# Denser cells, and the last two feed-forward groups in three float32r parts, in a fused mLSTM and feed-forward kernel

## The chip, the cores and the metric

One core of one Trainium2 chip runs the whole kernel in one launch. The metric is device time in microseconds (us). The core's engines are TensorE (PE; its weight loads are listed apart as PEld), VectorE (DVE), ScalarE (ACT), GpSimd (POOL) and SyncE (SP), which here issues nearly all DMAs. Each engine works through its own queue in order.

## The reference

```python
def _attn_ref(q, k, v, i_gate, f_gate, o_gate):          # q, k, v, o: (4, 8, 768, 40); gates: (4, 8, 768)
    for t in range(S):
        m_new = np.maximum(f_gate[:, :, t] + m, i_gate[:, :, t])
        f_stab = np.exp(f_gate[:, :, t] + m - m_new)
        i_stab = np.exp(i_gate[:, :, t] - m_new)
        m = m_new
        C = f_stab[:, :, None, None] * C + i_stab[:, :, None, None] * np.einsum('bhd,bhe->bhde', vt, kt)
        n = f_stab[:, :, None] * n + i_stab[:, :, None] * kt
        h_tilde = np.einsum('bhde,bhe->bhd', C, qt)
        denom = np.maximum(np.abs(np.einsum('bhd,bhd->bh', n, qt)[:, :, None]), 1.0)
        y[:, :, t] = 1.0 / (1.0 + np.exp(-o_gate[:, :, t])) * h_tilde / denom

def _moe_ref(x, w_in, w_out):                            # x: (3072, 320), w_in: (320, 2048), w_out: (2048, 320)
    h = x @ w_in
    g = np.maximum(0.01 * h, h)
    return (g @ w_out).astype(np.float32)
```

The cell's output, transposed to tokens by 8 x 40 features, is x. All is float32, except that the two weights come as float64.

## The kernel before

The sequence of 768 is cut into six chunks of 128 tokens (c = 0 to 5). With four batches (B = 4) there are 24 steps, s = 4 c + b. Inside a chunk the recurrence is worked in parallel form: decay weights (`gates`, `gates_exp`, `prep_mask`, `prep_exp`), scores and state products (`u_parts`), and the outputs (`u_plain` in chunk 1, `u_mix` in chunks 2 to 5). `u_mix` ends with VectorE transposes, a GpSimd multiplication and four DMAs that write the step's x, transposed, to memory (`x_dr`); `gather_x` reads it back in the layout that the feed-forward needs, with features on the partitions: two halves of 64 partitions and five slots (`SLOTS`), so that two row halves of TensorE can run side by side.

The feed-forward group g works on the 4 x 128 tokens of chunk g: `ff_units(g)` gives 32 pieces. The first 16 are half-units of the input product (`rows`, L743: products of 64 rows x 128 weight columns with 512 token columns into `ph`; ScalarE's Prelu, L751, writes `acts`). The last 16 are `part(n, m)` (L778: four products of 128 x 128 with 320 columns into `po`; after the fourth part ScalarE copies `po` out, L786, and a DMA stores it). All these products are float32. Weights arrive as 64-bit words and are narrowed by ScalarE and VectorE (`narrow_weights`, L231 to L247) in chunk 1.

The order of the work on TensorE, VectorE, ScalarE and GpSimd is the program's own order (a manual schedule); SP's DMAs are ordered by the framework, which also inserts all waits. After `first_chunk`, the loop over c = 1 to 6 goes through the 32 pieces of group c - 1 and puts the cells of chunk c between them: in chunks 2 to 5 at the pieces in

```python
        pairs = (2, 2, 6, 6, 14, 14, 19, 19, 19)
```

that is `u_parts` of two steps behind piece 2, their `u_mix` behind piece 6, the next two steps behind 14 and 19. After a `u_mix`, `ahead(s + 2)` prepares a later step (VectorE's `prep_kq`, GpSimd's `prep_vu`, DMAs for the step after it), `feed(s + NL)` loads the step that reuses its buffers, and from the middle of the group on `gather_x` runs. `masks` sets where GpSimd adds the causal mask (`prep_mask`, L434). Group 5 runs alone at the end, since there are no more cells.

Of the kernel before, what the change touches and what calls it, by code (L numbers as in the profile page):

```python
# [9 lines left out]
F32 = mybir.dt.float32  # L10
U32 = mybir.dt.uint32
# [3 lines left out]
PSUM = bass.MemoryType.PSUM  # L15


@with_exitstack
def kernel(
# [51 lines left out]
    assert KR == DP and KC == 5 and KC * DP == Dm and GT * 4 <= 2048  # L71

    consts = ctx.enter_context(tc.tile_pool(name="consts", bufs=1))
    gp = ctx.enter_context(tc.tile_pool(name="gates", bufs=1))
    wk = ctx.enter_context(tc.tile_pool(name="wk", bufs=2))
    psf = ctx.enter_context(tc.tile_pool(name="psf", bufs=4, space=PSUM))
    psc = ctx.enter_context(tc.tile_pool(name="psc", bufs=4, space=PSUM))
# [38 lines left out]
    NL = 4  # L116
# [8 lines left out]
    acts = consts.tile([P, NF, GT], F32, name="acts")  # L125
# [36 lines left out]
    QN = NF // 4  # L162
    QC = 4 * P
    WC = KC * 2 * P
    w_in = consts.tile([P, QN, WC], F32, name="w_in")
    w_out = consts.tile([P, NF, Dm], F32, name="w_out")
# [5 lines left out]
    def w_row(r, slot, j):  # L172
        n, e = divmod(j, 2)
        at = (2 * slot + e) * P
        return w_in[DP * r : DP * (r + 1), n, at : at + P]
# [6 lines left out]
    HW = 2 * Dm  # L182
    wide = moe_w_in.dtype == U64
    raws = {}
    if wide:
        raw_t = consts.tile([P, 5 * HW], U64, name="raw")

    def load_weights(n):

        m = n - QN  # L190
        if n < QN:
            dst = w_in[:, n, :]
        else:
            dst = w_out[:, 2 * m : 2 * m + 2, :].rearrange("p a d -> p (a d)")
        to = dst
        if wide:
            if n < 2:
                at = NF * GT - 2 * WC * (n + 1)
                raw = acts_l[:, at : at + 2 * WC].bitcast(U64)
            elif n < QN:  # L200
                raw = raw_t[:, WC * (n - 2) : WC * (n - 1)]
            elif m < 2:
                raw = w_out[:].rearrange("p f d -> p (f d)")[:, (2 + m) * WC : (3 + m) * WC].bitcast(U64)
            else:
                at = (4, 0, 1, 2, 3, 4)[m - 2] * HW
                raw = raw_t[:, at : at + HW]
            raws[n] = (raw, dst)
            to = raw
# [11 lines left out]
    def narrow_weights(n):  # L220
# [3 lines left out]
        if not wide:  # L224
            return
# [491 lines left out]
    def u_x(s):  # L717
# [3 lines left out]
        if b == 0:  # L721
            st["xT", c] = wk.tile([P, KC, GT], F32, name="xT", bufs=1)
# [308 lines left out]
```

## Time and profile before

| | us |
|---|---|
| median of 3 runs (lowest, highest) | 528.52 (527.25, 528.54) |
| profiled execution: its span from the first to the last instruction (the page gives it no other time) | 526.4 |
| TensorE busy in the span | 513.2 |
| VectorE, ScalarE, GpSimd busy | 240.3, 168.1, 113.0 |
| start of group 1's first product | 139.64 |
| start of group 5's first product | 453.96 |

A row of the page's fifth part, or of the groups by line, reads: line, engine, operation, written tile <- read tiles, shape, count | busy us, mean ns of one | idle time of the engine just before them, and who ended it. Durations of single instructions on TensorE overlap each other; what they cost in a row is read from the chain of waits, where the pieces stand in order of time with their start and length.

### The profile page before, as it was taken

What the parts mean: (1) busy time and instruction counts of PE and PEld (TensorE: products, weight loads), DVE (VectorE), ACT (ScalarE), POOL (GpSimd) and SP (SyncE); (2) the same over time, 40 slices, a digit from 0 to 9 for tenths busy, and PEclk for the clock granted to TensorE, in tenths of its full rate; (3) what the DMA queues carried; (4) which work ended last, traced back from release to release, by engine and by line L of the source; (5) the groups of instructions that cost most, each with busy time, mean ns of one, the idle gap of its engine ahead of it and who ended that gap; (6) DMA issues with size and microseconds to landing.
All of it is one profiled execution on the core that took longest, in us unless ns stands there. A gap on an engine that the chain in (4) does not pass through costs nothing.

```text
span 526.4 us, 11333 instructions
## 1 busy us (share of the span) xinstructions
PE 513.2 (97%) x4501; PEld 336.3 (64%) x4501; DVE 240.3 (46%) x431; ACT 168.1 (32%) x458; POOL 113.0 (21%) x145
## 2 busy tenths in 40 slices
PE   8889989999999999999999999999999999999997
PEld 7877878777555577555577555577554577544675
DVE  4679998999328446028445028344028230000000
ACT  4565865534534212034212124212125100122100
POOL 4244354152205121015021015021013010000000
PEclk9668999999999999999999999999999999999999
DMA  9977687888755626685626676626542112000000
GB/s 116 156 204 153 138 212 171 196 145 175 146 137 105 137 72 150 129 174 107 138 75 143 134 150 129 138 76 155 125 102 52 50 52 87 14 0 1 12 12 25
DMA packets 165284, 59.13 MB, mean 112 GB/s; under 512 B 128816, under 2 KB 156016, under 8 KB 165232
## 3 DMA queue, kind: packets, MB, share of 16 engines
q1 hardware_dynamic: 164848, 58.28, 51.0%
q8 instruction: 35, 0.57, 0.5%
q10 hardware_dynamic: 384, 0.13, 0.1%
q14 instruction: 17, 0.14, 0.1%
HBM read 51.68 MB, written 6.70 MB: 111 GB/s over the span
## 4 chain that ended last, share of the span: by engine, by line
PE 83%; SPq 6%; DVE 4%; DMA 2%; ACT 2%; issue 1%; POOL 1%; ACTq 0%; POOLq 0%
PE po L778 38%; PE ph L743 36%; PE pT L679 3%; SPq L213 3%; PE sd L598 3%; SPq L338 2%; SPq L352 1%; PE sd L603 1%; DMA rb<-in_q_dram 1%; DVE raw L245 1%; DVE qn L608 1%; DMA S<-in_v_dram 0%; DMA raw<-in_moe_w_in_dram 0%; PE tk L518 0%; PE hN L649 0%
## 5 line engine op out<-in xcount | busy, mean ns | idle before, releaser
L743 PE MATMUL ph<-xT,w_in 64*128 64x512 f32 (+1 forms) x1120 | 215.2, 536 | 0.6 <-ACT acts L751 0.6
L778 PE MATMUL po<-w_out,acts 128*128 128x320 f32 x768 | 211.1, 434 | 0.0
L778 PEld LDWEIGHTS po<-w_out,acts 128*128 128x128 f32 x768 | 144.5, 190 | 62.6 <-issue 4.1
L743 PEld LDWEIGHTS ph<-xT,w_in 64*128 64x128 f32 x1120 | 107.8, 189 | 94.4 <-issue 87.7
L751 ACT ACTIVATE acts<-ph 128x512 f32<-128x512 f32 (+1 forms) x112 | 53.9, 534 | 151.8 <-PE ph L743 151.7
L608 DVE TENSOR_TENSOR qn<-w,sd 64x512 f32<-64x512 f32 x40 | 27.4, 684 | 97.7 <-PE sd L603 57.1
L576 POOL TENSOR_TENSOR S<-S,f 40x336 f32<-40x336 f32 x36 | 30.9, 858 | 101.9 <-PE pT L679 65.8
L442 ACT ACTIVATE w<-w,gT 128x64 f32<-128x64 f32 (+1 forms) x192 | 51.1, 348 | 3.1 <-POOL w L434 2.1
L434 POOL TENSOR_TENSOR w<-w,i 128x512 f32<-128x512 f32 x20 | 28.1, 1411 | 104.7 <-ACT bu L294 53.0
L786 ACT COPY y<-po 128x320 f32<-128x320 f32 x12 | 5.1, 423 | 83.3 <-PE po L778 83.3
L786 ACT COPY hn<-po 128x320 f32<-128x320 f32 x12 | 5.1, 426 | 76.0 <-PE po L778 76.0
L686 DVE STREAM_TRANSPOSE hb<-pT 128x512 f32<-128x512 f32 x16 | 11.4, 714 | 39.2 <-PE pT L679 39.0
L495 DVE TENSOR_TENSOR qn<-kqT,ea 64x512 f32<-64x512 f32 x32 | 27.3, 854 | 0.9
L693 POOL TENSOR_TENSOR xb<-xb,den 128x320 f32<-128x320 f32 x16 | 11.7, 728 | 66.5 <-DVE xb L690 66.5
L598 PEld LDWEIGHTS sd<-kqT 40*64 40x64 f32 x640 | 19.9, 135 | 6.1 <-issue 6.1
L697 DVE STREAM_TRANSPOSE x<-xb 128x512 f32<-128x512 f32 x16 | 18.1, 1130 | 7.7 <-POOL xb L693 7.7
L598 PE MATMUL sd<-kqT 40*64 40x64 f32 x640 | 21.5, 220 | 0.0
L603 PE MATMUL sd<-S,vu 64*40 64x42 f32 x576 | 20.1, 214 | 0.7 <-POOL vu L462 0.7
L489 DVE STREAM_TRANSPOSE kqT<-rb 128x512 f32<-128x512 f32 x32 | 20.5, 677 | 0.0
L603 PEld LDWEIGHTS sd<-S,vu 64*40 64x40 f32 x576 | 18.6, 111 | 0.8 <-POOL vu L462 0.8
L580 DVE TENSOR_TENSOR S<-S,sd 40x336 f32<-40x336 f32 x36 | 18.1, 503 | 1.0
L679 PEld LDWEIGHTS pT<-qn,S 128*64 128x64 f32 x512 | 15.6, 138 | 3.6 <-issue 3.5
(126 smaller groups left out, 364.9 us busy)
## 6 DMA issues: line engine op xcount, KB each, us to landing
w<-a_dr SPq DMA_DIRECT2D x40, 128.0 KB
rb<-in_k_dram SPq DMA_DIRECT2D x64, 80.0 KB
rb<-in_q_dram SPq DMA_DIRECT2D x64, 80.0 KB
rb<-in_o_gate_dram SPq DMA_DIRECT2D x64, 80.0 KB
ea<-a_dr SPq DMA_DIRECT2D x32, 128.0 KB
kn<-in_k_dram SPq DMA_DIRECT2D x24, 160.0 KB
raw<-in_moe_w_out_dram SPq DMA_DIRECT2D x6, 640.0 KB
S<-in_v_dram SPq DMA_DIRECT2D x80, 40.0 KB
```

The source lines that it names most:

```text
L434: nc.gpsimd.tensor_tensor(w, w, cm2.unsqueeze(1).to_broadcast([P, H, SL]), op=ALU.add)
L442: yield nc.scalar.activation(w[:, h, :], w[:, h, :], AF.Exp, bias=gT[c][:, 0, bh : bh + 1], scale=1.0)
L489: nc.vector.transpose(d["kqT"][:, i].rearrange("p (h t n) -> p h n t", n=TS, t=QW), raw_blocks(s, i, QW).rearrange("p (h n) d -> p h n d", ...
L495: nc.vector.tensor_tensor(mixed(s)[rows, 1 - r], d["kqT"][rows, 1].rearrange("p (h t) -> p h t", t=SL), d["ea"][rows], op=ALU.mult,)
L576: nc.gpsimd.tensor_tensor(new, old, g, op=ALU.mult)
L598: nc.tensor.matmul(bank[1 - u][toks, h, :], lhsT=kqT[rows, 0, ts(h, SL)], rhs=kqT[rows, 1, ts(h, SL)], start=True, stop=True,)
L603: nc.tensor.matmul(dC[u][:, h].rearrange("p k d -> p (k d)"), lhsT=d["ku"][toks, h], rhs=S_v[s % NL][toks, u, h, :, :V1], start=True, stop ...
L608: nc.vector.tensor_tensor(mixed(s)[toks, u], w[toks], bank[1 - u][toks], op=ALU.mult)
L679: nc.tensor.matmul(pT[DP * r : DP * (r + 1), j * P + u * SL : j * P + (u + 1) * SL], lhsT=S[:, u, h, :], rhs=m[:, u, h, :], start=True, st ...
L743: nc.tensor.matmul(ph[r][:, cols], lhsT=w_row(r, slot, j), rhs=xT[DP * r : DP * (r + 1), slot, cols], start=(slot == 0), stop=(slot == KC ...
L751: nc.scalar.activation(acts[:, f, cols], ph[r][:, cols], AF.Prelu, alpha=0.01)
L778: nc.tensor.matmul(po[n][:], lhsT=acts[:, f, ts(n, P)], rhs=w_out[:, f, :], start=(f == 0), stop=(f == NF - 1),)
```

## The change

Four things are changed.

1. Cells of chunks 2 to 5 come among 24 pieces (`UC`) instead of 32, at (2, 2, 7, 7, 13, 13, 18, 18, 18). The pieces of groups 1 to 3 are simply counted on, so 96 pieces hold four chunks; in chunk 5 the loop ends behind piece 18, and the last five pieces of group 3 follow without cells. `gather_x` goes to other places.
2. v is loaded by one DMA instead of four, into the tile of the decay weights `w`, and GpSimd copies it from there into `S` (two copies in `prep_mask`). The spread of the weights (`spread`, `spread_q`) is one DMA instead of two each.
3. When the cells are done their tiles are given up, and groups 4 and 5 are worked as four half-groups (hg 8 to 11) of 256 tokens, in units of two row blocks (8 units a half-group, `enter` and `leave`). x and w_in, and from hg 9 on also the activations and w_out, are written as three float32r tensors each: a number is split by a bit mask into a high part and a rest, and three products (v = 0, 1, 2) into two PSUM sums are joined afterwards (`JOIN`).
4. The weights are split by `split_w`, in halves of 640 columns: one quarter of w_in in chunk 3, the other seven quarters (three of w_in, four of w_out) from the last five pieces of group 3 on, in steps between the units of hg 8. Two units' products are issued in a row: `enter(u)`, `enter(u + 1)`, then `leave(u - 2)`, `leave(u - 1)`.

```diff
-        for u in range(2):
-            for i in range(2):
-                nc.sync.dma_start(S_v[n][ts(u, SL), u, :, i, :DB], v[b, :, ...].rearrange("h p d -> p h d"))
+        w = wk.tile([P, H, P], F32, name="w", bufs=NL)[:].rearrange("p h t -> p (h t)")
+        ...
+        nc.sync.dma_start(w[:, H * SL : H * SL + Dm].rearrange("p (h d) -> p h d", d=D), v[b, :, rows, :].rearrange("h p d -> p h d"))
...
         w = st[s]["w"]
+        for u in range(2):
+            nc.gpsimd.tensor_copy(S_v[s % NL][ts(u, SL), u, :, :, :DB], st[s]["v"][ts(u, SL)])
         nc.gpsimd.tensor_tensor(w, w, cm2.unsqueeze(1).to_broadcast([P, H, SL]), op=ALU.add)
...
-        pairs = (2, 2, 6, 6, 14, 14, 19, 19, 19)
+        pairs = (2, 2, 7, 7, 13, 13, 18, 18, 18)
+        UC = 24
+
+        def split_w(w, parts):
+            tmp = raw_b[:].bitcast(F32)
+            n = WC // 2
+            for i in range(2):
+                at = slice(n * i, n * (i + 1))
+                h, low = (tmp[:, n * (2 * i + k) : n * (2 * i + k + 1)] for k in range(2))
+                nc.vector.tensor_scalar(h.bitcast(U32), w[:, at].bitcast(U32), scalar1=HIGH, scalar2=None, op0=ALU.bitwise_and)
+                yield
+                nc.scalar.copy(parts[0][:, at], h)
+                nc.gpsimd.tensor_tensor(low, w[:, at], h, op=ALU.subtract)
+                yield
+                nc.scalar.activation(parts[1][:, at], low, AF.Copy, scale=SPLIT)
+                yield
+                nc.vector.scalar_tensor_tensor(parts[2][:, at], in0=low, scalar=SPLIT, in1=h, op0=ALU.mult, op1=ALU.subtract)
+                yield
...
+        for c in range(2, NB):
+            cells, done, fed = cell_units(c), 0, 0
+            for i in range(UC):
+                ...
+                if c == 3:
+                    if i == 2:
+                        now = split_in(0)
+                    if i >= 2 and i % 2 == 0:
+                        run(now, 1)
+                ffs[at]()
+                at += 1
+                ...
+                visits(c, i)
+                ...
+                if c == NB - 1 and i == pairs[-1]:
+                    break
+
+        cell.close()
...
+        def split_x(hg):
+            to = xs[hg % 2]
+            for at, n in ((0, 3), (3, 2)):
+                ...
+                nc.vector.tensor_scalar(h.bitcast(U32), x.bitcast(U32), scalar1=HIGH, scalar2=None, op0=ALU.bitwise_and)
+                nc.scalar.copy(to[0][:, at : at + n, :], h)
+                nc.gpsimd.tensor_tensor(to[1][:, at : at + n, :], x, h, op=ALU.subtract)
+                nc.vector.scalar_tensor_tensor(to[2][:, at : at + n, :], in0=h, scalar=JOIN, in1=x, op0=ALU.mult, op1=ALU.subtract)
+                yield
...
+        load_x(HG0)
+        first = split_x(HG0)
+        now = splits()
+        while at < len(ffs):
+            ffs[at]()
+            at += 1
+            run(first, 1)
+            run(now, 4)
...
+        def enter(u):
+            ...
+            ph = psh.tile([P, 2, 2, GH], F32, name="p3")          # two buffers
+            for v in range(3):
+                for slot in range(KC):
+                    for r in range(2):
+                        nc.tensor.matmul(ph[:, r, v // 2, :], lhsT=w[rows, v, c0 : c0 + P], rhs=x[v][rows, slot, :], ...)
+            nc.scalar.activation(a, ph[:, :, 0, :], AF.Copy, scale=JOIN)
+            nc.vector.tensor_tensor(a, a, ph[:, :, 1, :], op=ALU.add)
+            nc.scalar.activation(a, a, AF.Prelu, alpha=0.01)
+
+        def grow(u):
+            ...
+            nc.vector.tensor_scalar(h.bitcast(U32), a.bitcast(U32), scalar1=HIGH, scalar2=None, op0=ALU.bitwise_and)
+            nc.scalar.copy(g[:, 0], h)
+            nc.vector.tensor_tensor(g[:, 1], a, h, op=ALU.subtract)
+            nc.vector.scalar_tensor_tensor(g[:, 2], in0=h, scalar=JOIN, in1=a, op0=ALU.mult, op1=ALU.subtract)
+
+        def leave(u):
+            # hg 8: one float32 product of 320 columns for each of 2 token halves and 2 row blocks;
+            # hg 9 to 11: three float32r products each; after a half-group's last unit the sums are joined and stored
+            ...
+
+        for u in range(HG0 * NJ, HG2 * NJ + LAG, 2):
+            hg, j = divmod(u, NJ)
+            for i in range(2):
+                if HG1 * NJ < u <= HG2 * NJ:
+                    grow(u - 2 + i)
+            for i in range(2):
+                if hg < HG1:
+                    run(now, 8)
+                if u < HG2 * NJ:
+                    enter(u + i)
+            if hg + 1 < HG2:
+                if j == 2:
+                    first = split_x(hg + 1)
+                if j in (2, 4):
+                    run(first, 1)
+                if j == 4 and hg + 2 < HG2:
+                    run(first, 1)
+                    load_x(hg + 2)
+            for i in range(2):
+                if u >= HG0 * NJ + LAG:
+                    leave(u - LAG + i)
```

## The prediction

> **What bounds the kernel now.** The page first, then the chain of waits in order of time, then groups by shape, single lines with their shortest, median and longest instruction, and the timelines of VectorE and GpSimd where the cells end.
>
> ```profile
> PE 513.2 (97%) x4501; PEld 336.3 (64%) x4501; DVE 240.3 (46%) x431; ACT 168.1 (32%) x458; POOL 113.0 (21%) x145
> PE   8889989999999999999999999999999999999997
> DVE  4679998999328446028445028344028230000000
> PEclk9668999999999999999999999999999999999999
> ```
>
> TensorE is the bound: full in every slice from the ninth on. VectorE's zeros at the right end are the room that the change wants to use.
>
> ```profile
> 139.64 7.07 PE ph L743 x32
> ...
> 218.46 7.07 PE ph L743 x32
> ...
> 375.99 7.07 PE ph L743 x32
> ...
> 427.99 26.04 PE po L778 x96
> 454.03 34.53 PE ph L743 x160
> 488.56 34.66 PE po L778 x128
> ```
>
> This is the chain. A group with a chunk's cells among its pieces takes 218.46 - 139.64 = 78.8 us, the one with the last chunk 454.03 - 375.99 = 78.0. A group alone takes 34.53 + 34.66 = 69.2: 16 half-units of ph and 16 parts of po at 2.16 us. So cells cost TensorE 9.6 us a chunk (the last 8.85), and the last matmul ends 526.4 - 523.2 = 3.2 us before the end. Moving cells among pieces gains TensorE nothing; it has to be given cheaper products.
>
> ```profile
> L778 PE MATMUL po<-w_out,acts 128*128 128x320 f32 x768 | 211.1, 434 | 0.0
> L743 PE MATMUL ph<-xT,w_in 64*128 64x512 f32 x800 | 176.3, 593 | 0.0
> L434 POOL TENSOR_TENSOR w<-w,i 128x512 f32<-128x512 f32 x20 | 28.1, 1411 | 104.7 <-ACT bu L294 53.0 <-DMA w<-a_dr 50.7 <-ACT w L442 1.0
> L243 DVE TENSOR_SCALAR raw<-w_out x6: 495/500/898, 94.0 to 126.8; 128x640 uint32<-128x640 uint32 x6
> L241 DVE SCALAR_TENSOR_TENSOR w_out<-raw,w_out x6: 824/825/1775, 92.2 to 125.9; 128x640 uint32<-128x640 uint32 x6
> L434 POOL TENSOR_TENSOR w<-w,i x20: 1262/1274/1764, 51.5 to 389.8; 128x512 f32<-128x512 f32 x20
> ```
>
> These are the prices. The two counts, 768 and 800, are twice the products written: a float32 product is two instructions. Without overlap a po product of 320 columns takes 34.66 / 64 = 542 ns and a ph product of 512 columns 34.53 / 80 = 432 (two row halves run side by side).
>
> ```profile
> 429.06 0.73 POOL L693 TENSOR_TENSOR xb<-xb,den 128x320 f32<-128x320 f32 x1 [23.28 <-DVE xb L690]
> 433.05 0.73 POOL L693 TENSOR_TENSOR xb<-xb,den 128x320 f32<-128x320 f32 x1 [3.27 <-DVE xb L690]
> 433.81 1.10 DVE L697 STREAM_TRANSPOSE x<-xb 128x512 f32<-128x512 f32 x1 [0.84 <-POOL xb L693]
> ```
>
> After the last cell matmul (427.99) VectorE still works until 434.9. GpSimd starts 0.08 to 0.14 us after VectorE hands over, VectorE 0.03 after GpSimd.
>
> **Part 1, when the cells are done (T0).** Up to 139.6 little changes. v comes by one DMA for four and the spread by one for two, against two GpSimd copies per step (nearest row 0.73, 1.5 a step). TensorE idles 3.4 us between 40 and 140, so the gain is at most 3.4; four uncovered steps would lose 6. I take 0. Behind that, 91 pieces and four chunks' cells: 139.6 + 3 x 69.2 - 5 x 2.17 + 3 x 9.63 + 8.85 = 374.1 = T0, against 428.0 before. The work per chunk is as before, in about 61.5 us instead of 78.8. VectorE needs 13 us for a pair of u_mix (316.2 to 329.2) and the next u_parts comes six pieces (13.0 us) later: just enough. SP issued without a pause from 353.0 to 386.5 behind a pair of u_mix; without four v DMAs, two spreads and most gathers that is some 22. I take 1 us in all, bounds 0 and 20 (5 a chunk).
>
> **Part 2, the products.** No row shows float32r. The nearest is the float32 product, two instructions; three float32r products cost between 3/4 of it (a quarter each, 54 ns for a ph product of 256 columns, 135 for po) and 3/2 (half each, what one of the two instructions takes); three times a whole one is the far end. I take a quarter. Then a unit of two row blocks takes 30 x 54 = 1.62 us in and 12 x 135 = 1.63 out, where float32 takes 2.16 each; a half-group takes 13.0 for 17.3. Nothing waiting, from T0: five pieces 10.8, hg 8 13.0 + 17.3 (its output stays float32), hg 9 to 11 26 each, together 119.1, and the span 374.1 + 119.1 + 3.2 = 496.4. That is the 30 us that the change is after.
>
> The trace hides the 128-row weight loads (190 ns) wholly behind products of the same rows: two po instructions take the 542. The Trainium skill, "TensorE: Matmul & The Clock Gate", part 3 "What overlaps and what doesn't", says that a load overlaps a running matmul only where their row groups differ, which speaks against short products. By it, with its 107 ns a load, an output product would be an estimated 242 for 135 and the whole up to 31 us later (107 ns x 12 x 24 units); the rows contradict it, and I keep the 135. "FP8 and Floating Point Precision", "TensorE Precision Notes", gives true FP32 four passes and lets reduced FP32 be truncated; one pass would be the quarter, and no row here shows it.
>
> **Part 3, the splitting, which decides.** A weight quarter is split in two halves of 640 columns: VectorE masks (0.50, L243), GpSimd subtracts (1.274 x 640/512 = 1.59, L434), VectorE joins (0.83, L241). In the order that the changed program issues, the next mask stands behind the join on VectorE's queue and the join waits for GpSimd. So a half takes 0.50 + 1.59 + 0.83 + 0.16 of hand-overs = 3.1 us, one after another. ScalarE's two copies (0.79 each, L231) fit beside. w_in's first quarter is split in chunk 3; seven quarters, 14 halves, are left at T0, and VectorE comes to them 6.9 us later, behind the last u_mix. x's two pieces come in between: 0.59 + 0.99 + 0.40 + 0.66, and GpSimd's part of them holds the halves up some 0.5: 3.2.
>
> The first add out of PSUM (0.69) has x and seven halves before it on VectorE, the next three two more each. ScalarE's scaled copy (0.59, L751) also stands in program order behind the halves; with the add it is 1.3. The adds end at T0 + 6.9 + 3.2 + 21.7 + 1.3 = 33.1, then, 6.2 + 1.3 later each, at 40.6, 48.1 and 55.6. PSUM has two buffers for enter, so units 66 to 69 wait for just these adds: behind the stalled enter stand all later products, and TensorE, which would be at unit 66 after 14 us, idles. After the fourth add TensorE still has enter(69) 1.6, two leaves 4.3, two enters 3.2, two leaves 4.3, two enters 3.2, two leaves 4.3, to T0 + 76.7; with nothing waiting this point is 10.8 + 13.0 + 17.3 + 3.2 = 44.3. Loss 32.
>
> **Part 4, hg 9 to 11.** A round of two units costs TensorE 6.5. VectorE does twice mask 0.43, subtract 0.69, join 0.69 and add 0.69 (512 columns; L608 and L495 0.69). Its second add waits for ScalarE's activation and next scaled copy of 0.59 each, in ScalarE's order: 3.6 + 0.69 + 0.59 + 0.59 + 0.69 + 0.5 of hand-overs = 6.65. Twelve rounds are 79.8, two further x splits 5.3, output adds 2.9: 88 against TensorE's 75. The gain of these products, 13, is eaten by the engine that prepares them.
>
> **The sum.** 374.1 + 76.7 + 88.0, then copy, add and store 3.7 (3.2 plus an add of 0.5): 542.5; 1 for part 1 and 2 for x's tiles, which reuse memory whose last stores may still be on their way (0 to 3). Span 545.5. The page gives the profiled execution by its span alone, 526.4; the median run is 528.5, 2.1 above. So 548.
>
> **Rivals.**
> *The preparing engines keep up.* Order and counts are fixed; open is only the price of a half, since no row subtracts two plain tensors of 640 columns on GpSimd. From T0 on 171 us are forecast (3 of them for parts 1 and 2) and 152.3 would be break-even: 13 halves would have to take 1.6 us each instead of 3.1. With the subtraction at nothing they take 1.4, TensorE is through hg 8 at T0 + 55, and the span 524, time 526; if the rounds of part 4 then also go at TensorE's 6.5, 514 and 516. Against it: L434's shortest of 20 is 1262 ns for fewer columns, and the mask and the join alone are 1.3. Faster by over 0.3%, 0.10 (about 500 to 526); between, 0.02.
> *float32r at half a float32 product.* Unit 3.24 in, 3.25 out, a round 13: TensorE bounds again. T0 + 84, twelve rounds 156, 3.7: 618, time 620; at the far end near 790. 0.09.
> *The dense cells starve TensorE.* 5 us a chunk: 565 to 570. 0.07.
> *The forecast,* 536 to 562 (a half at 2.8 to 3.4 is 4 either way, hand-overs in part 4 another 6, part 1 -3 to +6): 0.72.
>
> The range, 530 to 582, holds the forecast and the starving with something for their sum; the two outer rivals, 0.19, stay outside. 0.3% (1.6 us) is about what a measurement of this kernel tells from no change: faster 0.10, same 0.02, slower 0.88.
>
> **What would show it.** Right: the u_mix of chunk 5 ends near 374; behind it TensorE has some 15 us of idle time ended by VectorE's add, then 6 us gaps; VectorE is idle between mask and join, released by GpSimd; there a granted clock below 1.0, as PEclk's second and third slices have (0.6); VectorE at 9 tenths and more in the last 90 us. Wrong: if products of 256 columns follow each other at over 60 ns in the middle of a unit, part 2 fails; if the 14 halves last under 30 us, part 3 fails; if group 1 to 3 pieces show gaps, part 1.

## The result, and the profile after

| | before | after |
|---|---|---|
| median us (lowest, highest) | 528.53 (527.25, 529.76) | 651.00 (650.49, 653.68) |
| ratio after / before (95% interval) | | 1.233 (1.229 to 1.237) |
| span of the profiled execution, us | 526.4 | 651.9 |
| mean granted TensorE clock in it | 0.976 | 0.895 |
| last product of a cell ends (T0), us | 427.99 | 479.45 |
| from there to the end of the span, us | 98.4 | 172.4 |

The change costs 23%. The forecast was 548, with 582 as the upper end. Its two halves came out very differently: from T0 on 171.4 us were forecast and 172.4 measured, but T0 itself was forecast at 374.1 and came at 479.45. The whole miss, 105 us, lies in the stretch of the cells. It begins early: group 1's first product starts at 169.5, where it started at 139.6 before and the forecast had "little changes". From 139.6 to T0 TensorE stands idle for 77 us (0 before) at a mean granted clock of 0.87 (1.00 before). The other 28 us, by difference, are longer busy time; how much of them the clock makes, no run separates.

The page of after, one row of busy times and three rows of slices (16.3 us each):

```profile
PE 523.2 (80%) x5237; PEld 393.3 (60%) x5237; DVE 346.1 (53%) x589; ACT 230.1 (35%) x554; POOL 175.3 (27%) x209
...
PE   8877899944599996293399995796794269999997
...
DVE  5697989564038371260083730621635444587875
...
PEclk9678999978699999598599997989698589999999
```

Before, TensorE was full from the ninth slice on. Here it has holes of its own from the ninth slice to the 29th, all of them before T0 (the 30th slice), and the clock row falls to 5 to 8 tenths in these slices or the next ones. The dip that the forecast expected, behind T0, is there too (slices 31 to 33).

The waits of after, the longest that are not an engine's ordinary wait for its input:

```profile
POOL S L445 <- DMA w<-in_v_dram: 87.6, 9, 24.0
...
POOL w L446 <- DMA w<-a_dr: 57.1, 11, 14.0
...
ACT y L798 <- DMA out_dram<-y: 46.8, 3, 28.6
...
ACT wi L973 <- POOL raw_b L971: 35.9, 8, 28.9
```

The columns are total, count and longest, in us. None of these is TensorE, but what stands behind a waiting instruction on its queue can be something TensorE needs. The timeline of after shows two places, one on SP's queue and one on ScalarE's:

```profile
255.08 2.98 SPq L409 DMA_DIRECT2D w<-a_dr  x1
258.16 0.55 SPq L799 DMA_DIRECT2D out_dram<-y  x1
258.81 10.80 SPq L722 DMA_DIRECT2D xT<-x_dr  x12
...
266.29 0.43 ACT L798 COPY y<-po 128x320 f32<-128x320 f32 x1 [28.62 <-DMA out_dram<-y]
...
272.88 16.00 PE L758 MATMUL ph<-xT,w_in 64*128 64x512 f32 x60 [17.64 <-DMA xT<-x_dr]
...
301.62 0.95 POOL L445 COPY S<-w 64x320 f32<-64x320 f32 x2 [19.34 <-DMA w<-in_v_dram]
...
318.43 0.74 ACT L973 ACTIVATE wi<-raw_b 128x640 fp32r<-128x640 f32 x1 [28.92 <-POOL raw_b L971]
...
319.71 5.78 PE L758 MATMUL ph<-xT,w_in 64*128 64x512 f32 x12 [20.04 <-ACT acts L766]
```

First place: an output store (L799) gets its turn on SP at 258.16, behind a broadcast whose issue alone took 2.98 us. ScalarE stands 28.6 us with a finished sum that has no tile to go to. The gathers of the next group's x (L722) stand on SP behind that store, and it is they that end TensorE's 17.6 us. Second place: GpSimd waits 19.3 us for v. Behind v's copies and the masks stands GpSimd's part of the first weight split (L971). ScalarE's copy of that split (L973) waits 28.9 us, and behind it stand the Prelus (L766) that free the PSUM banks. TensorE is idle for 20.0.

The tail is read in the chain that ended last:

```profile
500.47 1.55 POOL raw_b L971
502.05 0.83 DVE wi L975
503.42 1.54 POOL raw_b L971
...
536.12 0.70 DVE ar L1155
...
572.76 3.71 PE so L1189 x24
576.47 3.78 PE p L1150 x58
```

The halves of the split follow one another every 2.94 us, GpSimd and VectorE by turns, up to the fourth add at 536.12. After that TensorE itself is most of the chain: 60 products in 3.78 and 24 in 3.71 us.

### The profile page after: what moved, and what is told of

Its sections match the earlier page's. It is cut to its first block, busy times and chain, and to the rows that moved or that the text cites. A ratio compares the mean times of both kernels' runs of the same rounds, so it can differ in the third digit from the quotient of the medians.

```text
span 651.9 us, 13080 instructions
## 1 busy us (share of the span) xinstructions
PE 523.2 (80%) x5237; PEld 393.3 (60%) x5237; DVE 346.1 (53%) x589; ACT 230.1 (35%) x554; POOL 175.3 (27%) x209
## 4 chain that ended last, share of the span: by engine, by line
PE 29%; DVE 7%; DMA 5%; POOL 5%; issue 2%; SPq 2%; ACT 1%; POOLq 0%; DVEq 0%; ACTq 0%
PE so L1189 8%; PE po L793 7%; PE p L1150 6%; PE ph L758 5%; DMA w<-a_dr 3%; POOL raw_b L971 3%; DMA w<-in_v_dram 1%; PE sd L610 1%; DVE raw_b L966 1%; PE pT L691 1%; DVE kqT L501 1%; SPq L358 1%; DVE h L1169 1%; DVE wi L975 1%; POOL xb L705 1%
## 5 line engine op out<-in xcount | busy, mean ns | idle before, releaser
L758 PE MATMUL ph<-xT,w_in 64*128 64x512 f32 (+1 forms) x800 | 158.0, 546 | 59.8 <-ACT acts L766 27.0
L793 PE MATMUL po<-w_out,acts 128*128 128x320 f32 x512 | 146.2, 443 | 9.3 <-DVE w_out L260 9.3
L793 PEld LDWEIGHTS po<-w_out,acts 128*128 128x128 f32 x512 | 97.3, 194 | 51.3 <-DVE w_out L260 10.3
L1150 PE MATMUL p<-xs,wi 64*128 64x256 f32 x960 | 68.2, 300 | 27.2 <-DVE xa L1155 18.3
L1150 PEld LDWEIGHTS p<-xs,wi 64*128 64x128 f32 x960 | 64.0, 203 | 32.4 <-DVE xa L1155 18.8
L766 ACT ACTIVATE acts<-ph 128x512 f32<-128x512 f32 (+1 forms) x80 | 36.6, 509 | 85.6 <-PE ph L758 85.4
L1189 PE MATMUL so<-wo,g 128*128 128x320 f32 x288 | 45.5, 314 | 0.1
L445 POOL COPY S<-w 64x320 f32<-64x320 f32 x40 | 21.1, 528 | 88.8 <-DMA w<-in_v_dram 87.6
L1189 PEld LDWEIGHTS so<-wo,g 128*128 128x128 f32 x288 | 42.3, 188 | 2.1 <-DVE g L1172 0.3
L1113 POOL TENSOR_TENSOR xs<-xa,xh 128x768 fp32r<-128x768 f32 (+1 forms) x8 | 17.0, 2131 | 65.7 <-DVE xh L1111 65.7
L709 DVE STREAM_TRANSPOSE x<-xb 128x512 f32<-128x512 f32 x16 | 17.8, 1112 | 21.7 <-POOL xb L705 21.7
```

What stands on the lines that cost most here:

```text
L445: nc.gpsimd.tensor_copy(S_v[s % NL][ts(u, SL), u, :, :, :DB], st[s]["v"][ts(u, SL)])
L758: nc.tensor.matmul(ph[r][:, cols], lhsT=w_row(r, slot, j), rhs=xT[DP * r : DP * (r + 1), slot, cols], start=(slot == 0), stop=(slot == KC ...
L766: nc.scalar.activation(acts[:, f, cols], ph[r][:, cols], AF.Prelu, alpha=0.01)
L793: nc.tensor.matmul(po[n][:], lhsT=acts[:, f, ts(n, P)], rhs=w_out[:, f, :], start=(f == 0), stop=(f == NF - 1),)
L1150: nc.tensor.matmul(ph[:, r, v // 2, :], lhsT=w[rows, v, c0 : c0 + P], rhs=x[v][rows, slot, :], start=(slot == 0 and v != 1), stop=(slot == ...
L1189: nc.tensor.matmul(p[:, v // 2, :Dm], lhsT=lhsT, rhs=rhs, start=(j == 0 and r == 0 and v != 1), stop=(j == NJ - 1 and r == 1 and (whole or ...
```

## Experiments: why the cells end late

Three theories stood at the start: the broadcast in one DMA is slow and holds up what is queued behind it (mine, after reading the two traces); the two output tiles that the change leaves block ScalarE; 24 pieces a chunk are too few for the cells.

T0 and the tail are read from each profiled run alike, T0 as the end of the last `pT` product. A kernel given without an interval ran once. Four kernels that are alike up to T0 but for the splits and x's gathers among the last pieces (E9 to E12) have T0 at 380.7, 376.2, 380.9 and 380.7, so 4 or 5 us between two single runs tell nothing.

| | | time | T0 | tail |
|---|---|---|---|---|
| after | | 651.0 | 479.5 | 172.4 |
| E1 | after, broadcasts in two DMAs | 573.1 | 399.2 | 172.0 |
| E2 | after, four output tiles | 634.1 | 458.6 | 173.7 |
| E3 | E1 and E2 together, and v by four DMAs | 584.9 | 410.4 | 172.7 |
| E5 | E1 and E2 together | 568.7 | 394.9 | 172.0 |
| E6 | E5, gathers spread, first split moved | 559.2 | 380.2 | 177.2 |
| E15 | after, masks later | 637.5 | 463.3 | 172.4 |
| before | | 528.5 | 428.0 | 98.4 |
| E4 | before, broadcasts in one DMA | 606.2 | 505.8 | 98.4 |
| E13 | before, two DMAs cut by heads | 636.3 | 536.0 | 98.5 |
| E14 | before, two output tiles | 580.5 | 480.1 | 98.5 |
| E17 | E14, stores on ScalarE's queue | 563.0 | 462.8 | 98.4 |

**E1 and E4, the broadcast.** The decay rows go to 128 partitions, the first 64 with one half of the chunk, the others with the second. The change writes this as one DMA over a pattern [2, 64, 512]; before it was two over [64, 512].

```diff
-        src = a_dr[c, 0, :, b * H : (b + 1) * H, :].rearrange("u h t -> u (h t)").unsqueeze(1).to_broadcast([2, SL, H * SL])
-        nc.sync.dma_start(d["w"].rearrange("p h t -> p (h t)"), src)
+        for u in range(2):
+            nc.sync.dma_start(d["w"][ts(u, SL)], a_dr[c, 0, u, b * H : (b + 1) * H, :].partition_broadcast(SL))
```

(`ea` alike.) E4 makes the reverse edit in the kernel before; like after, it and E13 also write `ea`'s rows with two DMAs for one, which E1 keeps.

> The changed kernel with each broadcast of the row terms to 128 partitions (w and ea) issued again as two DMAs of 64 partitions, as in the kernel before; all else as changed. Theory one (the broadcast in one DMA is slow, 2048-byte packets at 25 per us in the trace of after where the kernel before had 80 to 85, and holds up everything queued behind it): the cells of chunks 2 to 5 lose most of their waits, POOL's idle time before the copies of v (87.6 us, ended by w<-in_v) falls below 35 us, the last mix comes at 400 to 430 us where it came at 479, and the time is 575 to 605 us where it was 651. Theory two (two output buffers where there were four block ScalarE): at most 20 us less, above 630. Theory three (24 pieces a chunk are simply too few for the cells, whatever the DMAs do): 640 to 651.

> The kernel before with one edit: both broadcasts in one DMA each, as the change has them. 32 pieces a chunk, four output tiles and direct v stay. Theory one (the one-DMA broadcast is slow in itself): 2048-byte packets fall to 20 to 30 per us while a broadcast is on, and the kernel takes 540 to 590 us where it took 528.5, the less the more the longer chunks hide. Theory two or three (it costs nothing by itself): 526 to 532.

E1 takes 78 us off after, E4 adds 78 to before: theory one, and by more than it had. In E4 the longest new wait is one of the two that lead in after, GpSimd's mask for `w<-a_dr`: 146.4 us in all, against 50.7 before. The bytes are the same; what differs is how many DMA engines move them. Counted in the packet records from 140 us on, the microseconds with at least ten 2048-byte packets of a broadcast have up to 25 packets (90th percentile) at 84 ns each (their median) in after and in E4, 25 x 0.084 = 2.1 engines' worth, and some 80 in before and E1. There are 162 such microseconds in after and 68 before. Laid over one another in time, the packets say it more directly: of the time in which any of them is in flight, exactly 2 are for 89% in after and 90% in E4; in before it is 5 to 12 for two thirds of the time, and at times 16.

**E13, shape or number.** Two DMAs again, but each over four heads and both halves of the partitions, so over [2, 64, 256]:

```diff
+        for n in range(2):
+            src = a_dr[c, 0, :, b * H + n * PR : b * H + (n + 1) * PR, :].rearrange("u h t -> u (h t)")
+            src = src.unsqueeze(1).to_broadcast([2, SL, PR * SL])
+            nc.sync.dma_start(d["w"][:, n * PR : (n + 1) * PR].rearrange("p h t -> p (h t)"), src)
```

> The kernel before with each broadcast in two DMAs as it has them, but cut by heads where it cuts by halves of the chunk: each of the two still spans both halves of the partitions, so that its outer dimension is 2 as in the one DMA of the change (606 us in the kernel before). If the shape decides (an outer dimension of 2 leaves a broadcast to two of the 16 DMA engines), the packets land as slowly and the time is 585 to 610. If the number of DMAs decides (one transfer is served by few engines, two by twice as many), it is half way or better: 528 to 570.

The shape decides. Two DMAs of this shape are worse than one (636 against 606): packets of 1024 bytes, up to 46 per us at 46 ns, which is again 2.1 engines' worth and no more bytes per us, with exactly 2 in flight for 77% of the time. The Trainium skill, "DMA: Bandwidth & Descriptors", section "Why a DMA increments its semaphore by 16 and not by 1", says that a copy runs on the largest number of engines, up to 16, that divides the slowest dimension which is not 1 in both patterns; its "Rules for kernel authors" name a leading broadcast of c copies, confined to at most c engines. By it [2, 64, ...] gets 2, and the packets agree; [64, ...] gets 16. There the packets show 80 per us at 84 ns (their median) to 125 (their mean), 7 to 10 engines' worth, and at times 16 in flight, which agrees too.

**E2, E14 and E17, the output tiles.** A part of the change that the forecast did not price: the four sums of a group go to memory through two tiles `y` instead of two `y` and two `hn`. (In both kernels one of the cells' own operands, `qs`, goes through the two `y` as well.)

```diff
-                y = fp.tile([P, Dm], F32, name="y", bufs=2)[:]
+                if n < 2 or "pool" in three:
+                    y = fp.tile([P, Dm], F32, name="y", bufs=2)[:]
+                else:
+                    y = wk.tile([P, H, D1], F32, name="hn")[:].rearrange("p h d -> p (h d)")[:, :Dm]
```

> The changed kernel with four tiles for the dense outputs again (two y, two hn) where it has two; the broadcasts in one DMA and v by way of POOL stay. Theory one (slow broadcasts are the root, the output buffers only pass the delay on): the three waits of ScalarE for out_dram<-y (46.8 us) shrink below 10, but TensorE then waits for the cells in the same places, and the time falls by 5 to 25 us, to 626 to 646. Theory two (the buffers are the root): a fall of 30 to 60 us, to 591 to 621. Theory three (too few pieces a chunk): within 5 us of 651.

> The kernel before with all four dense outputs of a group in two tiles, as the change has them. In after ScalarE's wait for an output tile cost 17 us (651 to 634 with four), and 4 us where the broadcasts were mended (573 to 569). If a tile is late only because the store stands behind held up transfers on SP, the kernel before loses 0 to 4 us: 528 to 533. If two tiles are too few in themselves, 535 or more.

E2 gave what theory one had, 17 us. E14 missed: two tiles alone cost the kernel before 52 us. Its timeline, in the second of four such places:

```profile
220.33 5.68 SPq L714 DMA_DIRECT2D xT<-x_dr  x8
...
239.38 1.01 SPq L784 DMA_DIRECT2D out_dram<-y  x2
...
242.56 0.43 ACT L783 COPY y<-po 128x320 f32<-128x320 f32 x1 [21.42 <-DMA out_dram<-y]
```

(Of the four waits, 75 us in all, three are 21.4 to 21.5 and one 10.8.) SP issues gathers and the next chunk's loads from 220 to 239 and only then the stores. In before, with the same order on SP but four tiles, no wait of ScalarE for a store is among the longest; with two, ScalarE stands until a store has landed, and the Prelus behind it. So my expectation was wrong: a store behind *ordinary* loads is late enough.

```diff
-                nc.sync.dma_start(out[n * S + g * P : n * S + (g + 1) * P, :], y)
+                nc.scalar.dma_start(out[n * S + g * P : n * S + (g + 1) * P, :], y)
```

> The kernel before with two output tiles, as in the run that took 580 us, and with the stores of the outputs issued from ScalarE's own DMA queue, right behind the copy, where SP issues them. There ScalarE waited four times for a store, 21.4 us each, and the store stood on SP behind the next chunk's loads. If SP's order is what makes two tiles too few, the waits go and the time is 527 to 534. If a store itself takes long to land beside the loads, 555 or more.

Only half an answer, 563. With the stores on ScalarE's own queue its waits for them are gone (75 us to none), so SP's order was their cause. But now SP's loads wait for stores on the other queue (`SPq L382`, `L405` and `L714` for `out_dram<-y`, 23.5, 21.7 and 10.6 us), and TensorE waits three times 8.8 us, twice for a gather by the profile; the third wait's end it doesn't name. Why SP waits for those stores, and what the rest of the 35 us is, stays open.

**E3 and E5, v.** E5 is E1 and E2 together; E3 also loads v as before:

```diff
-        nc.sync.dma_start(w[:, H * SL : H * SL + Dm].rearrange("p (h d) -> p h d", d=D), v[b, :, rows, :].rearrange("h p d -> p h d"))
+        for u in range(2):
+            for i in range(2):
+                nc.sync.dma_start(S_v[n][ts(u, SL), u, :, i, :DB], v[b, :, ...].rearrange("h p d -> p h d"))
```

> The changed kernel with all three side edits undone together: broadcasts in two DMAs, four output tiles, and v loaded straight into the state tile by four DMAs with no copies on POOL; the 24 pieces a chunk, the split of the first weight block in chunk 3 and the whole tail stay. The forecast's step for the cells (last mix at 374, 0 to 20 us of stalls) holds for the spacing alone if the stalls came from these edits: last mix at 374 to 395, the time 548 to 570. Theory three (too few pieces a chunk): last mix above 430, the time above 605.

> The changed kernel with the broadcasts in two DMAs and four output tiles; v still comes in one DMA and is copied on POOL, as changed. With the broadcasts alone undone it took 573 us, with all three undone 585. If v in four DMAs costs SP's queue more than it saves POOL, this run is the best of the three: ScalarE's wait for an output tile near 230 us (4.7 us, TensorE idle 7.8) goes, the last mix starts its transpose at 388 to 398 where it was 402, and the time is 558 to 570. If the output tiles are what made that other run slower, it is 580 to 590.

E3 missed its 548 to 570 and E5 met its numbers: v by one DMA and two copies is the better way in this kernel, T0 394.9 against 410.4. With it there are 143918 packets, with the four DMAs 165357. This side edit of the change is a gain, where the forecast took 0.

**E6, the rest of the stretch.** E5 with chunk 2's gathers at units 16 and 17 of chunk 2 and 2 and 4 of chunk 3 (in the change in a row at its end), and with the first weight quarter split behind the cells, in `splits`, not in chunk 3.

```diff
-                if c == 2 and i >= UC - B:
-                    gather_x(2 * B + i - UC + B)
+                if (c, i) in ((2, 16), (2, 17), (3, 2), (3, 4)):
+                    gather_x(2 * B + ((2, 16), (2, 17), (3, 2), (3, 4)).index((c, i)))
...
-                if c == 3:
-                    if i == 2:
-                        now = split_in(0)
...
-            for n in range(1, QN):
+            for n in range(QN):
                 yield from split_in(n)
```

> The run above with two more edits in the cells' stretch: the 16 gathers of chunk 2's activations leave SP in two parts (units 16 and 17 of chunk 2, 2 and 4 of chunk 3) where they left in a row at its end, and the first weight block is split behind the cells where it was split in chunk 3. If TensorE's last stalls come from these (the gathers held up an output store and the first product of group 2; ScalarE waited 16 us for POOL's part of the split), the last mix's transpose starts at 376 to 388, which is what the forecast had for 24 pieces (374 and up to 20), and the time is that plus 170, plus 6 for the two halves moved: 552 to 566. If 24 pieces are too few for the cells themselves, it starts at 392 or later and the time is 570 or more.

T0 380.2, with nothing changed in the spacing. That closes the account for the 105 us: the broadcasts 80 (479.5 to 399.2), of which 27 lie ahead of group 1 (it starts at 142.1 in E1, for 169.5); the output tiles 4 behind them (394.9), no more than single runs differ by; gathers and the chunk 3 split, mended together, 15 (380.2); and 6 left between this and the forecast's 374.1. The parts do not add in any order: two output tiles move T0 by 4 us where the broadcasts are mended, by 21 where they are not, and by 52 in the kernel before.

**E15, GpSimd's order.** `masks` at units 8 and 19 where the change has 0 and 12, nothing else.

```diff
-        masks = {0: (2, 3), 12: (4, 5)}
+        masks = {8: (2, 3), 19: (4, 5)}
```

> The changed kernel with one edit: the copies of v and the masks of a chunk's steps come on GpSimd at units 8 and 19 (behind the mixes of units 7 and 18) where they come at units 0 and 12; the broadcasts stay in one DMA. If GpSimd's order turns late transfers into TensorE's idle time (its 88 and 57 us of waits for w<-in_v and w<-a_dr stand ahead of the mixes' and the split's work), the last mix's transpose comes 15 to 40 us earlier than 482, the time is 611 to 636. If the late transfers hold the exponentials and so the products in any order, within 8 us of 651, or slower where the masks are now too late themselves.

The last transpose starts 16 us earlier, the time is 13.5 less, 637.5: at the weak end of the first theory for the transpose, and just short of its 611 to 636 for the time. GpSimd's order passes on a part of the delay; most of it reaches TensorE in any order.

## Experiments: the tail, and a version that pays

**E7, halves one ahead.** E6, and `split_w` writes the next half's mask before the present half's join.

```diff
+            mask(0)
+            for k in range(len(halves)):
+                if k + 1 < len(halves):
+                    mask(k + 1)
+                ...   # copy, subtract, scaled copy and join of half k, in the old order
```

> The run above with the splits of the weights one half ahead: VectorE writes the mask of the next half before it joins the present one, so that GpSimd's 1.54 us no longer stands in series with VectorE's 0.49 and 0.82. Forecast's part 3 (the ramp behind the cells is a serial chain of halves, 2.94 us each in after, 16 of them here): halves every 1.6 to 2.0 us, the wait of TensorE before the tail's third product group falls by 12 to 18 us, the time by the same. Rival (the ramp is bound by something else, ScalarE or the loads of x): within 4 us of the run above.

The tail fell by 8.5 us (177.2 to 168.7), not by 12 to 18. A half still takes 2.48 us, and the timeline shows why; the order is the same in E10, whose lines these are:

```profile
363.94 3.22 POOL L991 TENSOR_TENSOR raw_b<-w_in,raw_b 128x640 f32<-128x640 f32 x2 [2.62 <-DVE raw_b L976]
...
365.69 2.15 DVE L995 SCALAR_TENSOR_TENSOR wi<-raw_b 128x640 fp32r<-128x640 f32 x1 [1.43 <-POOL raw_b L991]
...
386.96 0.82 DVE L995 SCALAR_TENSOR_TENSOR wi<-raw_b 128x640 fp32r<-128x640 f32 x1
...
387.19 2.00 POOL L991 TENSOR_TENSOR raw_b<-w_in,raw_b 128x640 f32<-128x640 f32 x1 [2.02 <-ACT wi L993]
...
387.88 1.66 DVE L976 TENSOR_SCALAR raw_b<-w_in 128x640 uint32<-128x640 uint32 x1
...
389.46 0.81 DVE L995 SCALAR_TENSOR_TENSOR wi<-raw_b 128x640 fp32r<-128x640 f32 x1
```

The mask (L976), 0.49 us alone, takes 1.66 beside GpSimd's subtraction (L991) and ends 0.35 behind it; the subtraction, 1.54 alone, takes 2.0 where VectorE's join (L995) is already under way, as at 386.96. That join takes its usual 0.82. Where the subtraction is first (the second of the two in the top line starts at 365.62), the join takes 2.15. Side by side the two engines hold each other up, and it is the later one that loses.

**E8, nothing on TensorE waits for a split.** E7, and the first half of group 4 (hg 8) in plain float32, both products; the splits run behind it.

```diff
+            if hg < HG1:
+                ...
+                nc.tensor.matmul(ph[:, r, 0, :], lhsT=w_row(r, slot, j), rhs=x8[DP * r : DP * (r + 1), slot, :], ...)
+                ...
+                nc.scalar.activation(a, ph[:, :, 0, :], AF.Prelu, alpha=0.01)
+                return
```

> The run above with the first half of group 4 in plain float32, both products, with the splits running behind it: nothing on TensorE waits for a split until the second half of group 4. By rows of after: five pieces left over 16 us, eight units at 2.17 and 2.25 us make 35, three halves of a group in three parts at 7.5 us a pair of units make 90, the end 3: 144 us behind the last mix. With the last mix at 376 to 388 the time is 522 to 535, against 528.2 of the kernel before. Rival (16 halves take over 55 us, or VectorE's order delays the first sums of group 4's second half): 10 to 20 us more.

533.8: the time is met, by an early T0 (379.1) and a tail of 152.9 where 144 was expected. TensorE was still idle 2.8 us for hg 8's x and some 2.6 us for sums that stood behind ScalarE's split copies.

**E9, the spacing alone.** The mended cells, and behind them groups 4 and 5 in plain float32 pieces; no float32r.

```diff
-        cell.close()
...
+        while True:
+            if at == len(ffs):
+                g, at = g + 1, 0
+                if g == NB:
+                    break
+                ffs = ff_units(g)
+            ffs[at]()
+            at += 1
...
```

> The mended cells' stretch (24 pieces a chunk, broadcasts in two DMAs, four output tiles, chunk 2's gathers at units 16, 17, 19 and 20) and behind it groups 4 and 5 in plain float32 pieces as the kernel before has them: the spacing alone, with no float32r part. The forecast took the spacing to cost nothing and bring nothing by itself: TensorE does the same work in another order, so the last mix's transpose at 374 to 382 and the time 524 to 532, level with the kernel before (528 to 529.5). If the closer cells cost TensorE by themselves (their products and loads between fewer pieces), 535 or more.

535.0, T0 380.7, tail 152.5. The time is 7 us above the kernel before, at the edge of the expectation's second case. The forecast's break-even, 152.3 behind T0, is what plain float32 takes. The spacing itself costs 6.6 us here (380.7 for 374.1; 2 to 7 over E9 to E12), inside its bounds of 0 to 20 but above the 1 that was taken.

**E10 and E11.** E10 is E8 with chunk 2's gathers at 16, 17, 19 and 20, hg 8's x fetched in chunk 5, the first quarter split there, and fewer splits ahead of the first sums. E11 also moves the subtraction.

```diff
+                if c == 2 and i in (16, 17, 19, 20):
+                    gather_x(2 * B + (16, 17, 19, 20).index(i))
+                if c == NB - 1 and i in (9, 11):
...
+                    gather(4 * B + (i - 9) // 2, xf, ts((i - 9) // 2, P))
+                if c == NB - 1 and 9 <= i < 17:
+                    run(now, 1)
...
-                    run(now, 6 if j < 6 else 4)
+                    run(now, (2, 4, 6, 6)[j // 2])
```

```diff
-                nc.gpsimd.tensor_tensor(low, w, h, op=ALU.subtract)
+                nc.vector.tensor_tensor(low, w, h, op=ALU.subtract)
```

> The run with the first half of group 4 in plain float32 (533.8 us), with three waits moved: chunk 2's last gathers in front of chunk 3's loads on SP (TensorE idle 3.6 us at 222 there), x of group 4 fetched in chunk 5 into the tile that group 3's activations leave (idle 2.8 at 390), and the first weight block split in chunk 5 with fewer splits before the first sums of the tail (idle 2.6 between 400 and 406). If these idle stretches are what is left between this version and the sum, 9 us go and some of the clock's slow restart with them: 522 to 527. If others take their place, 528 to 533.

> The same with the split's subtraction on VectorE where it is on GpSimd. In the pipelined splits VectorE's mask takes 1.64 us beside GpSimd's subtraction where it takes 0.49 alone, and the subtraction 1.98 where it takes 1.54 alone. If the two hold each other up by sharing a path, the half needs 2.2 us on VectorE (0.49, 0.86, 0.82) where it needs 2.48 now, and the time is 0 to 4 us less than the run before. If it is only the order of the queues, halves of 2.5 or more and no gain.

E10 met its numbers with 526.4 us. E11, 531.7, gave the price but no gain:

```profile
393.38 0.49 DVE L976 TENSOR_SCALAR raw_b<-w_in 128x640 uint32<-128x640 uint32 x1
393.79 0.82 DVE L991 TENSOR_TENSOR raw_b<-w_in,raw_b 128x640 f32<-128x640 f32 x1
```

All on VectorE, with no GpSimd beside, the mask is 0.49 again and a half takes 2.2 us. But the tail is 149.0 against 148.4: ScalarE's order set it, with 4.4 (E10) and 4.6 us (E11) of idle TensorE before hg 8's third unit, ended by the Prelu that stands behind the split copies. The 5 us by which E11 is longer lie before T0, and are no more than single runs differ by there. The Trainium skill, "SBUF — State Buffer", section "SBUF: two separate sides", describes the port pair that VectorE and GpSimd share as an exclusive lock that the instruction which starts first holds to its end; the mask's 0.49, 1.66 and 0.49 and the join's 0.82 and 2.15 fit that.

**E12, what a float32r product costs.** E10 with the middle one of the three parts over half the columns (128 coming in, 160 going out); the other half is left out.

```diff
+                        if v == 1:
+                            rhs = rhs[:, : Dm // 2]      # and : GH // 2 of x's columns in enter
```

> The kernel of e10 in which the middle of the three parts multiplies half the columns only (128 of 256 tokens coming in, 160 of 320 outputs going out; the other half of that part is left out of the sums). It sizes the float32r product, which the forecast had at 54 and 135 ns and the trace of after at 63 and 155. If the columns that stream set its time, a burst of 60 products falls from 3.85 us to 3.2 and one of 24 from 3.79 to 3.2. If the load of 128 weight columns before each product sets it, the bursts stay within 0.1 us; if a load costs a fixed part that nothing hides, in between.

The chain of E12:

```profile
500.02 3.43 PE so L1220 x24
503.45 3.68 PE p L1178 x60
```

In the chains of after and E18 these are 3.71 and 3.78. So 20 of the 60 products with half the columns save 0.10 us, 63 to 58 ns each (two row halves run side by side); 8 of 24 save 0.28, 155 to 120 each. Were columns all, each would have halved. Coming in, something that does not depend on the columns sets the time; going out, the line through the two points has 85 ns at no columns (an estimate from 120 at 160 and 155 at 320).

**E16 and E18.** E18 is E10 with fewer of the splits' steps ahead of hg 8's first sums; E16 has the later masks as well.

```diff
-                    run(now, (2, 4, 6, 6)[j // 2])
+                    run(now, (4, 4, 7, 8, 5)[(u - HG0 * NJ) // 2])      # and none between group 3's last pieces
```

> The kernel of e10 (526.4 us) with two orders changed: the masks at units 8 and 19, and in the first half of group 4 fewer steps of the splits ahead of the first sums on ScalarE (there TensorE was idle 4.4 us at 391, waiting for a sum that stood behind six of ScalarE's copies). TensorE is idle 1 to 2 us each at 220, 330 and 362 in e10, waiting for the cells. If these are what is left: 519 to 524, a ratio of 0.982 to 0.992 to the kernel before. If the splits then end too late for group 4's second half (14 halves of 2.48 us are 35 us, and so is TensorE's float32 half), 524 to 529.

> The kernel of e10 with the later splits in the first half of group 4 alone (the masks at units 0 and 12 as in e10; with them at 8 and 19 the last mix came 5 to 10 us later). The last mix's transpose at 379 to 384 and the 4.4 us of idle TensorE at 391 gone: 521 to 527, a ratio of 0.987 to 0.997. If the splits end too late for group 4's second half, 526 to 530.

E16 missed its 519 to 524: 529.64, ratio 1.0025 (0.9993 to 1.0057), with T0 at 387.0. Later masks helped where the broadcasts were late and hurt where they were not (E16 and E18 differ in the masks alone). E18: 524.35 against 528.01, ratio 0.990 (0.987 to 0.994). It is faster than both kernels. Its page's slices for TensorE (13.1 us each), and its chain behind T0:

```profile
PE   7879989999999999989999999998999999999997
```

```profile
423.91 3.79 PE p L1177 x60
427.70 4.50 PE so L1216 x16
432.20 3.79 PE p L1177 x60
436.00 3.71 PE so L1216 x24
```

TensorE has no hole left behind T0 (381.6), and the tail is 141.1 us, 11.4 less than plain float32 in E9. Some 7 us of that pay for the closer cells.

## Why the prediction was wrong, by its own steps

**Part 1 failed.** "I take 1 us in all, bounds 0 and 20" was 105, and "up to 139.6 little changes" was 30 of it. The closer cells, which this price was meant for, kept inside its bounds: 6 us in E6 (380.2 for 374.1). What failed stands beside it:

- "v comes by one DMA for four and the spread by one for two, against two GpSimd copies per step ... I take 0." I counted DMAs and GpSimd's copies and not how the one DMA is spread over engines, though the rule quoted at E13 speaks against just this edit. The spread cost 80 us of after (E1) and 78 in the kernel before (E4), against bounds of -3.4 and +6, which were drawn for the first 139.6 us alone; 27 of the 80 fell there, and for the rest the sum has no term for it. v by one DMA, its neighbour in the same sentence, was a gain (E3, E5).
- The two output tiles stand in the diff and in none of my terms. Every buffer that an edit takes away can turn a late store into a wait of the engine that fills it: 21.4 us three times in E14.
- "SP issued without a pause ... some 22" counted SP's queue by length. What matters more is its order: who stands behind what.

The rival "the dense cells starve TensorE" had most of the place right (gaps in groups 1 to 3, which the last paragraph named as the sign that part 1 fails) and both the cause and the size wrong: 5 us a chunk, 565 to 570.

**Part 2: size off.** Products of 54 and 135 ns were forecast, 63 and 155 measured, about 0.28 of a float32 product (226 ns coming in and 562 going out in hg 8 of E18) and not 0.25. By the sign that the text set, "over 60 ns in the middle of a unit", part 2 fails, by 3 ns. The runs lie above 135 and far below the estimated 242 that followed from the Trainium skill ("TensorE: Matmul & The Clock Gate", part 3), with its 107 ns for a load that is not hidden. With loads of 188 ns (the mean of L1189's records in after) and a product every 155, loads do run beside products of the same rows. I had inferred "wholly" from long products only; whether the 20 ns above 135 are the part that isn't hidden, no run shows.

**Part 3 held.** Halves every 2.94 us (forecast 3.1), GpSimd's subtraction 1.54 (1.59), the ends of the four adds at T0 + 36.3, 43.3, 50.3 and 57.4 (33.1, 40.6, 48.1, 55.6), the end of hg 8's outputs at T0 + 82.0 (76.7). E7 and E8 confirm it from the other side: shorter halves shorten the tail by 8.5 us, no need for them by 15.8 more.

**Part 4: right sum, wrong engine.** 86.6 us for hg 9 to 11 (88.0). But a round takes 7.5 on TensorE, and VectorE (7 to 8 tenths, not 9) was the chain only around the change of half-groups. Two errors met: products dearer than forecast, VectorE's 6.65 therefore hidden; 11 inputs at 3.78 and 12 outputs at 3.71 make 86.1 on TensorE. That the sum came out is luck.

The direction was forecast with 0.88, and the reason given for it, the splitting behind the cells, is real: E6, with the cells mended, is 559.2. By itself it would have put the time inside the range.

## What to carry to other kernels

Price a DMA by the shape of its pattern, not by its bytes or by the number of DMAs: one broadcast with an outer dimension of 2 in place of two with 64 cost 80 us here. For each edit that removes a buffer or adds a wait, list what stands behind it on that engine's queue and follow that to the bound engine; the engines that "have room" in the page were the ones that stopped TensorE. And when a forecast has parts, measure them apart: here the difficult part came out within 1 us, with some luck, and the one taken at nothing was off by 105.

## What was not expected of the hardware

- A broadcast over [2, 64, 512] moved with 2 packets in flight (25 per us at 84 ns), over [64, 512] with 5 to 12 most of the time (80 per us).
- VectorE's 128 x 640 mask takes 0.49 us alone and 1.66 beside a GpSimd subtraction of two tensors; its two-tensor join keeps its 0.82 when it starts first, and then the subtraction goes from 1.54 to 2.0, and takes 2.15 when the subtraction starts first.
- A float32r product of 64 rows, two row halves side by side, comes every 63 ns with 256 columns and still every 58 with 128; one of 128 rows 155 with 320 and 120 with 160.
